# Another order for the steps behind the first key tile of a linear-attention and feed-forward kernel

## The chip, the cores and the metric

The kernel runs on one core of one Trainium2 chip. The metric is the device time of one execution in microseconds (us); a lower one is better. A core has five engines, each with an instruction stream of its own, which wait for each other through semaphores: TensorE (PE in the profile, PEld its weight loads), VectorE (DVE), ScalarE (ACT), GpSimd (POOL) and SyncE (SP), which here issues nearly all transfers and transposing transfers.

## The reference

Two residual blocks over 2048 tokens of width 640, in bf16. The first is a linear attention with 32 heads of width 20, the second a feed-forward of width 1728 with SiLU.

```
q, k, v = split(layernorm(x) @ wqkv)          # 32 heads of 20
pq, pk  = q @ w_phi, k @ w_phi                # per head, 20 x 20
phi_q   = [softmax(pq), softmax(-pq)]         # 40 features
phi_k   = [softmax(pk), softmax(-pk)]
kv, z   = phi_k^T @ v, sum over tokens of phi_k
o       = (phi_q @ kv) / (phi_q . z + 1e-6)
h       = x + o @ wo
out     = h + silu(layernorm(h) @ w1) @ w2
```

## The kernel before

The 2048 tokens are 16 tiles of 128. The program is a list of 899 named steps (`ORDER`, lines 18 to 61). Each name stands for a small function that emits the instructions of one step; they are emitted in the order of the list (lines 1097 to 1102), and each engine runs its own instructions in that order. So the list fixes the order on every engine and on SP's queue. It is written out by hand, as far as the kernel is concerned: nothing reorders it later. The number in a name is the tile, or the unit of tiles.

The first stage folds `w_phi` into the query and key weights (`wk`, `fk`, `fq`: small products on PE; `wq` is a transposing load of a query weight block, `WTq`, line 425). Then, for each tile `t`:

- `st`, `rs`, `xn`: layer norm. `st` (lines 478, 479) on DVE; `rs` on ACT or POOL; `xn` (line 494) on DVE for tiles 0, 1, 2 and 6 and on POOL for the others.
- `xt`: transposes the normalized tile into `XnT`. For tiles 0 to 3 PE does it (line 530); from tile 4 on SP issues a transposing transfer (line 552).
- `K`, `V` (line 571, ten matmuls each): keys and values; `ex` (line 626, ACT), `su` (line 630, DVE), `rk` (lines 638, 639, ACT), `sc` (line 643, DVE) make the two softmaxes of the keys in the tile `EK`; `ve` (line 647, ACT) copies the values. `kv` (line 662, eleven matmuls on PE) adds the tile to the running key-value product and needs `sc` and `ve`.
- `Q` (line 609, ten matmuls), `qe` (line 733, ACT), `qs`, `ql`, `qi`, `qr`: the query features `EQ`; `qt` (line 779) issues their transposing transfer into `EqT`.
- `bd` (lines 671, 673, DVE) cuts the finished key-value product to blocks; `D` (line 817, PE) multiplies the query features by it, `E` (lines 826, 827, DVE) divides into the tile `O`, `ot` (line 839) issues its transposing transfer into `OT`, `G` (line 849, two halves) is the output projection and `ga` (line 856, DVE) the residual.
- `lm`, `ls`, `lr`, `hn`, `ht`: the second layer norm and its transposing transfer into `HnT`.

The feed-forward works on units of two or four tiles: `u` (lines 931, 942) and `s` (lines 954, 970) are the first product and SiLU, `lt` a transposing transfer. The second product takes tiles in pairs and multiplies blocks of a 2 by 2 split with seven products instead of eight: `T` and `S` (DVE) form sums of weights and of activations, `p1` to `p7` (line 1036) are the products, `r` and `w` (lines 1044, 1051) gather them, `out` stores. The last pair's `p3` is cut into 192 and 128 columns, `p3.14` and `p3.14x`.

The weights of the later stages come through eleven loads on SP (`load0` to `load10`, line 563): `load0` is `wo` (800 KB), `load1` to `load5` are `w1` (432 KB each), `load6` to `load8` (480 KB each), `load9` (640 KB) and `load10` (80 KB) are `w2`.

Results of PE go to eight PSUM banks. While keys and values are projected, three pairs of banks are taken in turn, so a `K`, `V`, `fq` or early `Q` also waits until the step that empties its pair three takings ago (`ex`, `ve`, `fq..e`, `qe`) has run. Later (from the step `halves` on) a ring of single banks is used in the same way.

Of the kernel before, what the change touches and what calls it, by code (L numbers as in the profile page):

```python
# [26 lines left out]
ve6 fq1 st10 fq1e K7 V7 zeros rs10 su5 xt8 rk4 sc4 fq4 xt9 ex7 ve7 rs11 kv4 fq4e ref8 ones6 xn10 su6 su7
rk5 V8 ve8 V9 load4 rk7 sc5 st12 fq5 ve9 st14 rk6 xn11 rs12 K8 fq5e xt10 ref9 rs13 xn12 ex8 sc6 kv5 sc7
K9 su8 ref10 load1 V10 ex9 ve10 load5 kv6 eqr0 rs14 su9 Q0 K10 rk8 xn13 kv7 Q1 xt12 qe0 ref11 xt11 sc8
rk9 ref12 st15 sc9 xt13 xn14 kv8 rs15 K12 kv9 ex10 V12 su10 qe1 ex12 load0 K11 qs1 ve12 K13 xt14 rk10  # L30
su12 ex11 load10 qs0 ref13 V11 sc10 kv10 xn15 ex13 xt15 K14 su11 ql1 ve11 eqr1 rk12 V13 su13 qi1 ref15
eqp rk11 sc11 ql0 ref14 K15 qr1 rk13 load8 mask1 sc12 ex14 ve13 sc13 ex15 kv11 load2 Q2 V15 V14 qe2 su14
qi0 su15 rk14 qr0 rk15 load3 ve14 Q3 qt1 ve15 sc14 kv12 kv13 sc15 kv14 qe3 kv15 Q7 qs2 ql2 qe7 qi2 bd0
Q5 halves qt0 bd1 D0 qr2 D1 qe5 qs3 load9 Q4 qt2 E0 qe4 ql3 Q10 qe10 D2 E1 qs5 qi3 qr3 Q6 qe6 ot0 ot1
G00 G01 ql5 qs4 E2 Q9 ql4 ga0 qi5 G11 qe9 qt3 G10 qr5 Q11 lm0 qi4 ls0 D3 qr4 ot2 lr0 qs6 ga1 Q8 qe11 lm1
G20 E3 qs7 qr6 G21 qt5 Q12 hn0 ls1 ot3 ga2 lr1 qt4 qe8 Q13 qr7 D5 G31 E5 G30 hn1 ht0 ht1 ga3 qe12 qs8
Q14 ot5 qe13 qt6 qe14 Q15 qe15 padL0 D4 T1.0 qr8 u0.L u0.8 padL1 T1.2 E4 G50 G51 qt7 T3.0 lm2 s0.L T1.1
ga5 s0.8 lm3 u0.10 s0.10 ls2 lm5 D6 T2.2 u0.4 u0.2 ot4 E6 D7 qs9 u0.6 u0.12 T3.2 s0.2 s0.4 E7 ls5 lr2
T2.0 lt0 u0.0 s0.6 G41 qr9 qt8 ot6 s0.12 G40 D8 s0.0 hn2 ot7 T2.1 p2.0 G61 T3.1 lr5 hn5 ga4 S1.0 p1.0
S3.0 ls3 S2.0 p7.0 G60 lr3 lm4 E8 ht5 r1.0 ls4 G71 S4.0 lr4 w11.0 p6.0 ga6 hn3 T4.1 p3.0 r2.0 hn4 r7.0  # L40
T4.0 G70 p5.0 T4.2 ht2 qs10 ht3 ga7 p4.0 lm7 r3.0 ht4 qt9 w21.0 lm6 w12.0 u2.L ls7 s2.L u2.3 u2.12 w22.0
D9 u2.0 u2.4 s2.12 u2.11 qs11 s2.0 ot8 s2.3 ls6 G81 G80 u2.7 qr10 qr11 E9 s2.11 u2.6 lr6 s2.6 qs14 s2.4
qt10 ga8 qs12 u2.5 qr12 lm8 u2.8 D10 out0 ot9 E10 qt11 s2.5 u2.10 hn6 ls8 G90 s2.7 u2.1 s2.8 s2.10 u2.9
out1 G91 qr14 u2.2 qs13 qr13 qt12 ga9 ot10 D11 s2.1 lt2 E11 ht6 s2.9 s2.2 S3.2 lm9 qt13 S1.2 ot11 lr8
hn8 ls9 p2.2 ht8 p1.2 lr7 D12 r1.2 S2.2 qt14 G101 G100 p7.2 p6.2 E12 r7.2 p4.2 lr9 hn7 ht7 G110 S4.2 hn9
ga10 S3.4 r2.2 w11.2 w21.2 G111 ot12 ga11 p7.4 p5.2 w22.2 lm10 r3.2 ht9 ls10 D13 lm11 ls11 p3.2 S1.4
p1.4 G121 S2.4 lr11 u6.1 r7.4 G120 r1.4 p6.4 w12.2 E13 p4.4 s6.1 ot13 ga12 D14 r2.4 w21.4 out3 E14 lm12
p5.4 ls12 lr12 u6.L w22.4 G131 r3.4 ot14 hn11 qs15 u6.3 G130 s6.L u6.2 qr15 u6.0 u6.9 ht11 s6.2 lr10
ga13 s6.0 p2.4 lm13 s6.9 w11.4 out5 hn12 u6.7 s6.3 hn10 G140 G141 u6.11 out2 s6.7 qt15 ht12 ls13 D15
S4.4 lr13 ht10 u6.12 u6.4 u6.10 s6.11 E15 ga14 hn13 s6.4 ht13 p3.4 w12.4 u6.5 u10.L ot15 s6.10 u6.8 s6.5  # L50
u6.6 s10.L lm14 s6.12 G151 s6.6 G150 lt6 S3.6 s6.8 S1.6 u10.2 ls14 p1.6 S2.6 r1.6 ga15 lm15 p7.6 r7.6
p6.6 u10.3 s10.2 p2.6 p4.6 S4.6 u10.6 s10.3 r2.6 p5.6 u10.8 u10.11 u10.9 lr14 s10.8 w21.6 S3.8 w22.6
r3.6 w11.6 p3.6 p7.8 hn14 p1.8 S1.8 s10.6 S2.8 ht14 u10.7 r1.8 p2.8 ls15 s10.9 p6.8 s10.11 s10.7 w11.8
lt10 w12.6 r7.8 u10.0 out4 u10.1 p4.8 r2.8 p5.8 lr15 u10.4 u10.10 r3.8 hn15 s10.0 w21.8 w22.8 u10.12
ht15 s10.4 s10.10 s10.12 u10.5 s10.1 u14.2 S4.8 s10.5 s14.2 S3.10 u14.12 u14.0 p2.10 out7 p7.10 S3.12
S1.10 s14.0 p3.8 p1.10 r7.10 S2.10 S4.10 out6 u14.10 p4.10 w12.8 s14.12 u14.L r1.10 u14.4 p6.10 s14.10
w11.10 p1.12 r2.10 p5.10 w21.10 u14.6 p7.12 w22.10 S1.12 s14.4 p2.12 s14.L r3.10 r7.12 r1.12 p3.10 S2.12
out8 s14.6 p4.12 w11.12 S3.14 p6.12 w12.10 out9 u14.8 s14.8 lt14 r2.12 w21.12 out11 p5.12 w22.12 p1.14
r3.12 S4.12 p7.14 S1.14 p3.12 out10 r7.14 S2.14 r1.14 p4.14 p6.14 out13 p2.14 S4.14 r2.14 w12.12 w11.14
w21.14 p5.14 p3.14 w22.14 out12 out140 r3.14 w12.14 out15 p3.14x out141 w12.14x out142  # L60
""".split()


# [1071 lines left out]
```

## Time and profile before

| | us |
|---|---|
| median of 3 runs | 227.71 (227.59 to 228.24) |
| profiled execution, its own time | 227.59 |
| its span in the profile | 225.7 |
| PE busy | 218.2 |
| DVE busy | 173.9 |
| ACT busy | 146.1 |
| POOL busy | 70.0 |

The span runs from the first to the last instruction of the trace; times inside it are counted from its start. The granted clock of TensorE was 0.999 of full speed. A row of a timeline gives the start, the time until the end of the last instruction of the row, engine, line, operation, tiles and the number of instructions; brackets hold the engine's idle time before the row and what ended it. In the rows of waits stand the waiting engine and line, what it waited for, the total in us, how often, and the longest.

### The profile page before, as it was taken

Reading aid. Unit: us, or ns where it says so; the run is one execution under the profiler, and the core shown is the slowest. Engines: PE = TensorE matmul, PEld = TensorE weight load, DVE = VectorE, ACT = ScalarE, POOL = GpSimd, SP = SyncE. Lnnn points to the kernel's source line nnn. Section 1 sums busy time; section 2 is a strip of 40 time slices with the busy share of each in tenths; the row PEclk is TensorE's granted clock in tenths of the full one; section 3 lists DMA queues with packets and bytes.
Section 4 is the critical chain, followed back from the end, with each engine's and each line's share of the span. In section 5 each row is a group of like instructions: output and inputs, shape, how many; then the busy total and the mean of one; then the engine's idle time right before and its main releaser. Section 6 shows DMA issues by size and latency. Waiting matters only on the chain.

```text
span 225.7 us, 5046 instructions
## 1 busy us (share of the span) xinstructions
PE 218.2 (97%) x1927; PEld 154.4 (68%) x1937; DVE 173.9 (77%) x305; ACT 146.1 (65%) x321; POOL 70.0 (31%) x136
## 2 busy tenths in 40 slices
PE   6899989999999999999999999999999999999994
PEld 5777767777777677887655577655556565777773
DVE  4999988999999999999998998881435533174674
ACT  2899979999988899988275776439473532612100
POOL 7589969897400131034010321130110010000000
PEclk9999999999999999999999999999999999999999
DMA  6999984669848659874735696245310033002002
GB/s 170 292 345 162 202 98 116 183 120 198 292 94 182 128 96 143 174 102 92 148 73 144 143 154 123 61 117 109 75 23 0 11 75 87 0 23 79 32 29 87
DMA packets 68158, 26.98 MB, mean 120 GB/s; under 512 B 61159, under 2 KB 67111, under 8 KB 68007
## 3 DMA queue, kind: packets, MB, share of 16 engines
q1 hardware_dynamic: 67479, 26.65, 54.3%
q8 instruction: 15, 0.25, 0.4%
q10 hardware_dynamic: 656, 0.03, 0.2%
q14 instruction: 8, 0.07, 0.1%
HBM read 9.55 MB, written 2.62 MB: 54 GB/s over the span
## 4 chain that ended last, share of the span: by engine, by line
PE 75%; DVE 14%; DMA 5%; issue 2%; ACT 2%; DVEq 0%; ACTq 0%
PE banks L931 25%; PE banks L1036 23%; PE banks L849 10%; PE banks L571 7%; PE banks L609 5%; DVE st L478 4%; DMA XnT<-xn 3%; PE banks L817 2%; DVE EK L643 2%; DVE Sk L630 2%; DMA OT<-O 2%; DVE Sq L737 1%; DVE xn L494 1%; PE banks L662 1%; ACT EK L626 1%
## 5 line engine op out<-in xcount | busy, mean ns | idle before, releaser
L931 PE MATMUL banks<-HnT,w_sb 128*128 128x512 bf16 (+1 forms) x315 | 59.8, 335 | 0.5
L954 ACT ACTIVATE shT<-banks 128x512 bf16<-128x512 f32 (+1 forms) x53 | 30.0, 587 | 45.2 <-PE banks L931 44.8
L931 PEld LDWEIGHTS <-w_sb 128*128 128x128 bf16 x325 | 31.2, 98 | 21.1
L571 PEld LDWEIGHTS <-XnT 128*128 128x128 bf16 x300 | 28.5, 98 | 10.9 <-DMA XnT<-xn 1.3
L494 POOL TENSOR_SCALAR xn<-X,mv,rs 128x640 bf16<-128x640 bf16 x12 | 30.8, 2565 | 1.5 <-ACT rs L485 1.3
L516 POOL TENSOR_SCALAR rs<-mv 128x1 f32<-128x1 f32 x16 | 4.7, 296 | 82.8 <-ACT xn L509 82.6
L1036 PEld LDWEIGHTS <-S 128*128 128x128 bf16 x231 | 22.1, 98 | 8.5
L1036 PE MATMUL banks<-T,S 128*128 128x320 bf16 x168 | 26.2, 299 | 0.0
L1051 DVE TENSOR_TENSOR o_t<-banks,r 128x320 bf16<-128x320 f32 (+2 forms) x33 | 15.1, 476 | 13.4 <-PE banks L1036 13.1
L849 PE MATMUL banks<-wo_sb,OT 128*128 128x320 bf16 x160 | 25.0, 299 | 0.4 <-DMA OT<-O 0.4
L1044 DVE TENSOR_TENSOR r<-banks,X 128x320 f32<-128x320 f32 x32 | 15.2, 485 | 12.9 <-PE banks L1036 12.8
L737 DVE TENSOR_REDUCE Sq<-EQ 128x66 f32<-128x1320 bf16 x16 | 24.3, 1519 | 0.0
L609 PE MATMUL banks<-Wfq,XnT 128*128 128x342 bf16 (+2 forms) x160 | 22.8, 293 | 0.0
L733 ACT ACTIVATE EQ<-banks 128x342 bf16<-128x342 f32 (+2 forms) x52 | 21.6, 527 | 1.9 <-PE banks L609 1.7
L571 PE MATMUL banks<-Wfk,XnT 128*128 128x304 bf16 x150 | 21.7, 292 | 1.0 <-DMA XnT<-xn 1.0
L571 PE MATMUL banks<-Wv,XnT 128*128 128x320 bf16 x150 | 22.5, 299 | 0.0
L630 DVE TENSOR_REDUCE Sk<-EK 128x64 f32<-128x1216 bf16 x16 | 21.9, 1402 | 0.4 <-ACT EK L626 0.4
L1036 PEld LDWEIGHTS <-shT 128*128 128x128 bf16 x168 | 16.3, 98 | 6.9
L626 ACT ACTIVATE EK<-banks 128x608 bf16<-128x608 f32 x32 | 20.3, 695 | 0.8 <-PE banks L571 0.8
L849 PEld LDWEIGHTS <-OT 128*128 128x128 bf16 x160 | 15.3, 98 | 7.4 <-DMA OT<-O 0.6
L609 PEld LDWEIGHTS <-XnT 128*128 128x128 bf16 x160 | 15.0, 97 | 5.4
L504 ACT ACTIVATE xn<-X 128x640 bf16<-128x640 bf16 x16 | 11.9, 745 | 10.0 <-DVE X L856 10.0
(97 smaller groups left out, 327.1 us busy)
## 6 DMA issues: line engine op xcount, KB each, us to landing
out_dram<-o_t SPq DMA_DIRECT2D x15, 160.0 KB, 1.9
w_sb<-in_B_w_dram SPq DMA_DIRECT2D x5, 432.0 KB, 3.8
w_sb<-in_B_w_dram SPq DMA_DIRECT2D x3, 480.0 KB, 4.1
X<-in_A_x_dram SPq DMA_DIRECT2D x1, 1280.0 KB, 8.0
Wk<-in_A_wqkv_dram SPq DMA_DIRECT2D x5, 160.0 KB, 3.6
Wv<-in_A_wqkv_dram SPq DMA_DIRECT2D x5, 160.0 KB, 5.2
wo_sb<-in_A_wo_dram SPq DMA_DIRECT2D x1, 800.0 KB, 6.3
X<-in_A_x_dram SPq DMA_DIRECT2D x1, 640.0 KB, 6.3
```

The lines of the kernel that those rows point to most:

```text
L494: eng.tensor_scalar(out=xn_[t][:], in0=X[:, t, :], scalar1=mv_.pop(t)[:, 0:1], scalar2=rs_.pop(t)[:], op0=ALU.subtract, op1=ALU.mult,)
L571: nc.tensor.matmul(ps[:, g, 0:w], XnT[:, c, t * P : (t + 1) * P], W[:, c, g * w : (g + 1) * w], start=(c == 0), stop=(c == C - 1),)
L609: nc.tensor.matmul(ps[:, 0 : e - a], XnT[:, c, t * P : (t + 1) * P], Wfq[:, c, a:e], start=(c == 0), stop=(c == C - 1),)
L626: nc.scalar.activation(E5[:, :, :, b, 0:DR], p4, AF.Exp, scale=sign)
L630: nc.vector.tensor_reduce(sk[t][:], ek[t][:, 0 : H * HF].rearrange("p (q f) -> p q f", f=DH)[:, :, 0:DR], axis=AX.X, op=ALU.add)
L733: nc.scalar.activation(features(t, a, b)[:, :, :, i, 0:DR], p4, AF.Exp, scale=sign)
L737: nc.vector.tensor_reduce(sq[t][:], EQ[0][:, t, :, 0:FCH].rearrange("p c (q f) -> p c q f", f=DH), axis=AX.X, op=ALU.add)
L849: nc.tensor.matmul(ps_of["G", t][:, g, 0:HD], ot[t][:, c, :], wo_sb[:, c, g * HD : (g + 1) * HD], start=(c == 0), stop=(c == C - 1),)
L931: nc.tensor.matmul(ps[:, at : at + n], w1_sb[:, c, fc * P : fc * P + P], HnT[u][:, c, 0:n], start=(c == 0), stop=(c == C - 1),)
L954: nc.scalar.activation(rows_of(u)[:, f0 * n : f1 * n], ps_of.pop(("u", u, f0))[:, 0 : (f1 - f0) * n], AF.Silu)
L1036: nc.tensor.matmul(ps[:, lo:hi], left[:, c, :], right[:, c, lo:hi], start=(c == 0 and k in FIRST), stop=(c == KS - 1 and k in LAST), skip_ ...
L1044: nc.vector.tensor_tensor(r_[t, name][:], ps_of[bank, t][:, 0:HD], X[:, t + i, g * HD : (g + 1) * HD], op=ALU.add)
```

## The change

The same 899 steps stand in the list in another order from the 105th on; the first that moves is `wq3`. No step is added, removed or altered, and no function changes. On SP's queue the order of the transposing transfers and the loads becomes another one, on PE, DVE, ACT and POOL that of the computing steps. What the prediction speaks of:

- SP before: `X8 wq3 wq2 wq0 xt4 load7 xt5 load6 xt6 wq1 xt7 wq5 xt8 xt9 load4 xt10 load1 load5 xt12 xt11 xt13 load0 xt14 load10 xt15 load8 load2 load3 qt1 qt0 load9 qt2 ot0 ot1`
- SP after: `X8 load10 wq0 xt4 wq3 xt5 xt6 wq2 xt7 wq1 xt8 xt9 wq5 xt12 xt10 load7 load3 xt11 load9 xt13 load1 xt14 load4 xt15 load0 load2 qt0 qt1 load8 load5 load6 qt2 ot0 ot1`
- PE before, from `V0.4`: `V2 K2 V3 K3 kv0 kv1 K4 V4 fq3 V5 fq0 K5 K6 fq2 kv2 kv3 V6 fq1 K7 V7 fq4 kv4 V8 V9 fq5 K8 kv5 K9 V10 kv6 Q0 K10 kv7 Q1`
- PE after: `K2 V2 V3 kv0 K3 K4 V4 kv1 fq0 V5 fq3 K5 K6 kv2 kv3 V6 fq2 K7 V7 kv4 fq1 V8 fq4 V9 K8 K9 fq5 kv5 kv6 kv7 Q0 K10 V10 Q1`
- PE around the first `G`, before: `D0 D1 Q4 Q10 D2 Q6 G00 G01 Q9`; after: `D0 D1 Q4 Q10 Q6 D2 Q9 G00 G01`
- DVE before, from `su0`: `su0 su1 st6 st7 sc0 xn6 sc1 st11 st8 su3 su2 sc3 st9 sc2 st13 su4 st10 su5 sc4 su6 su7 sc5 st12 st14 fq5e sc6 sc7`
- DVE after: `su0 st6 su1 sc0 st7 st9 xn6 sc1 st12 st8 su2 su3 st10 sc2 sc3 su4 su5 su6 sc4 st15 st11 su7 st14 sc6 sc5 sc7 fq5e`

The head of the diff:

```diff
-wph0 K0.4 rs3 rs2 st4 K0.3 K1 V0.2 xn2 xt2 st5 ex0 rs4 ex1 V0.1 wph1 x2 V1 X8 ve1 xn3 wq3 xt3 V0.4 x3
-wq2 xn4 wq0 rs5 ve0 xn5 su0 rk0 V2 su1 st6 st7 rs6 sc0 K2 V3 xn6 rk1 ve2 xt4 ones5 rs7 K3 sc1 st11 kv0
-ex2 st8 kv1 ve3 ex3 load7 phq xt5 ones2 K4 rs8 load6 su3 ex4 rk3 xt6 su2 wq1 sc3 V4 st9 ve4 fq3 fq3e rk2
-xn7 V5 ref5 ve5 sc2 fq0 fq0e st13 rs9 K5 ref6 ex5 xn8 K6 fq2 kv2 ref7 ex6 xt7 su4 fq2e xn9 kv3 wq5 V6
...
+wph0 K0.4 rs3 rs2 st4 K0.3 K1 V0.2 xn2 xt2 st5 ex0 rs4 ex1 V0.1 wph1 x2 V1 X8 ve1 xn3 xt3 su0 st6 rk0
+xn4 V0.4 su1 x3 load10 ones5 wq0 sc0 K2 st7 rs5 st9 ve0 V2 xn5 rs6 xt4 xn6 ex2 rk1 sc1 ve2 ones2 rs9
+st12 wq3 xt5 phq V3 kv0 rs7 ve3 xt6 K3 K4 xn7 V4 ref5 kv1 ex3 ex4 st8 rs8 su2 su3 ve4 fq0 fq0e V5 fq3
+ref6 st10 rk2 xn8 ve5 wq2 K5 xn9 rk3 xt7 fq3e sc2 ex5 K6 ex6 kv2 wq1 sc3 su4 kv3 ref7 V6 su5 fq2 rk4 ve6
...
```

The list ends, before, with `p3.14 w22.14 out12 out140 r3.14 w12.14 out15 p3.14x out141 w12.14x out142`, and after with `p3.14x w22.14 p3.14 r3.14 w12.14x out13 out140 out15 out142 w12.14 out141`.

More of the change, by code (lines that the diff above doesn't have):

```diff
@@ L27 @@
[L27 to L60, printed above, removed]
+wph0 K0.4 rs3 rs2 st4 K0.3 K1 V0.2 xn2 xt2 st5 ex0 rs4 ex1 V0.1 wph1 x2 V1 X8 ve1 xn3 xt3 su0 st6 rk0
@@ new lines @@
+xn4 V0.4 su1 x3 load10 ones5 wq0 sc0 K2 st7 rs5 st9 ve0 V2 xn5 rs6 xt4 xn6 ex2 rk1 sc1 ve2 ones2 rs9
+st12 wq3 xt5 phq V3 kv0 rs7 ve3 xt6 K3 K4 xn7 V4 ref5 kv1 ex3 ex4 st8 rs8 su2 su3 ve4 fq0 fq0e V5 fq3
+ref6 st10 rk2 xn8 ve5 wq2 K5 xn9 rk3 xt7 fq3e sc2 ex5 K6 ex6 kv2 wq1 sc3 su4 kv3 ref7 V6 su5 fq2 rk4 ve6
+K7 V7 rs12 fq2e ref8 su6 xn12 sc4 kv4 fq1 rs10 ex7 ve7 xt8 st15 rk6 ones6 xt9 fq1e zeros V8 st11 su7 fq4
+xn10 st14 ref9 ve8 rs11 wq5 sc6 rk5 fq4e xt12 xt10 rk7 V9 load7 sc5 ve9 K8 xn11 K9 sc7 fq5 kv5 fq5e kv6
@@ new lines @@
+load3 kv7 ex8 ex9 st13 rs14 rs13 eqr0 su8 Q0 qe0 su9 ref10 rk8 rk9 xn13 K10 ref12 xn14 ex10 xt11 V10 sc8
+ve10 ref11 load9 Q1 kv8 V12 rs15 xn15 xt13 K12 qs0 qe1 su10 sc9 kv9 rk10 ve12 ref13 K11 load1 ex12 K13
+ex11 sc10 qs1 su12 xt14 ql0 ex13 ql1 V11 su11 su13 eqr1 rk12 rk11 load4 qi0 ve11 kv10 K14 xt15 sc11 rk13
+V13 ref14 sc12 eqp qr0 qi1 ex14 ve13 qr1 sc13 ref15 K15 load0 Q2 ex15 load2 kv11 kv12 su14 kv13 su15 V15
+qe2 qt0 rk14 qt1 rk15 V14 sc14 ve14 sc15 mask1 load8 ve15 Q3 qs2 kv14 ql2 kv15 Q5 bd0 qe3 qe5 Q7 bd1
@@ new lines @@
+load5 qi2 halves qr2 qe7 D0 D1 qs3 ql3 E0 load6 Q4 qe4 Q10 qi3 qt2 E1 qr3 qs5 qe10 qs4 ql5 Q6 qe6 ot0 D2
+ot1 Q9 qe9 qi5 ql4 qr5 E2 G00 G01 ga0 lm0 ls0 qi4 G11 G10 qt3 Q11 qs6 qr4 D3 ga1 qe11 qt5 E3 lm1 lr0 hn0
+Q8 ls1 D5 ot2 qt4 Q13 qr6 G20 qs7 lr1 G21 qe8 hn1 Q14 qe13 E5 Q15 qe14 ot3 Q12 ga2 G31 G30 ht0 qe15 qe12
+padL0 qs8 ht1 D4 u0.L ot5 T1.2 T1.0 qr7 s0.L T1.1 u0.0 lm2 padL1 qt6 ga3 E4 qt7 u0.6 qs9 G50 s0.0 qr8
+lm3 G51 T2.1 s0.6 D6 u0.4 ls2 s0.4 ga5 E6 u0.8 D7 ot4 lr2 lm5 qt8 u0.10 T3.2 u0.2 E7 G41 G40 ls5 hn2
@@ new lines @@
+u0.12 ot6 s0.2 T2.2 D8 lr5 s0.8 T3.1 T3.0 lt0 ls3 S3.0 s0.10 ga4 hn5 E8 s0.12 ot7 T2.0 p7.0 S1.0 G61
+p1.0 T4.1 S2.0 p2.0 r1.0 r7.0 G60 ht2 p6.0 T4.0 T4.2 lr3 p4.0 G71 S4.0 r2.0 p3.0 lm4 p5.0 qr9 ls4 lr4
+G70 ga6 hn3 ht5 w21.0 qs11 hn4 w22.0 ga7 ht3 ht4 u2.L lm6 u2.9 s2.L u2.1 qt9 r3.0 u2.7 ot8 w11.0 lm7
+w12.0 lt2 qr11 u2.10 s2.9 qs10 G81 qt11 s2.1 qr10 qs12 D9 u2.3 s2.3 s2.7 qt10 G80 E9 u2.5 ls6 lr6 u2.4
+s2.10 u2.2 ga8 u2.6 D10 ls7 u2.0 ot9 qr12 qt12 qs13 u2.12 s2.4 E10 lm8 D11 hn6 s2.5 ls8 ot10 u2.8 s2.0
@@ new lines @@
+qs14 E11 s2.6 s2.12 lr7 lr8 u2.11 G90 qr13 s2.2 D12 hn7 hn8 S3.2 ht6 s2.8 G91 p7.2 G101 qr14 ga9 s2.11
+S1.2 p1.2 S2.2 E12 G100 r1.2 out0 p2.2 ga10 qt13 ot11 lm9 p6.2 qt14 S4.2 D13 r2.2 r7.2 G110 G111 w11.2
+ls9 out1 S3.4 p4.2 E13 p5.2 ot12 ga11 lr9 w21.2 ht7 hn9 ht9 ht8 w22.2 ot13 D14 p7.4 r3.2 E14 lm11 p3.2
+qs15 S1.4 p1.4 S2.4 ls11 G121 r1.4 lm10 u6.L ls10 G120 u6.8 lr10 p6.4 r7.4 p4.4 ga12 S4.4 r2.4 lm12 qr15
+G131 w12.2 ot14 w21.4 G130 ga13 qt15 s6.L hn10 ls12 ht10 p5.4 lr11 s6.8 u6.11 G140 lm13 hn11 s6.11 u6.4
@@ new lines @@
+s6.4 lr12 D15 G141 u6.2 hn12 ls13 out3 r3.4 w22.4 p2.4 u6.5 s6.5 s6.2 E15 ga14 lr13 hn13 u6.1 w11.4 ht12
+u6.0 u6.3 lt6 u6.10 u6.7 out2 s6.10 s6.7 s6.3 s6.1 p3.4 w12.4 ht11 ht13 u6.6 s6.0 u10.L ot15 u6.12 u10.2
+s6.12 u10.9 s10.L G151 G150 s6.6 u6.9 S3.6 s10.2 u10.11 s6.9 S1.6 ga15 S2.6 lm15 u10.0 p7.6 s10.9 p1.6
+u10.6 lt10 lm14 S3.8 r1.6 s10.0 r7.6 s10.11 u10.7 s10.6 s10.7 u10.12 p4.6 S4.6 p6.6 p2.6 s10.12 r2.6
+p5.6 r3.6 ls15 w11.6 w21.6 u10.5 p2.8 S1.8 ls14 u10.3 w22.6 out5 lr15 u10.1 s10.5 p7.8 lr14 p1.8 S2.8
@@ new lines @@
+s10.3 hn14 u10.4 hn15 s10.1 r1.8 s10.4 ht14 w11.8 S3.10 p3.6 p6.8 ht15 r7.8 S4.8 u10.8 p4.8 out4 u14.4
+r2.8 w21.8 w12.6 s14.4 u10.10 p5.8 s10.8 w22.8 p3.8 r3.8 out6 u14.2 out9 w12.8 s14.2 s10.10 S1.10 u14.12
+p7.10 u14.10 out7 u14.L s14.12 u14.0 u14.6 p1.10 out8 S3.12 s14.0 s14.L r7.10 lt14 u14.8 S2.10 r1.10
+s14.6 p6.10 p4.10 s14.10 r2.10 p5.10 w21.10 r3.10 S4.10 p2.10 p7.12 p2.12 w11.10 w22.10 S1.12 p1.12
+S2.12 r1.12 w11.12 p3.10 p6.12 r7.12 p4.12 S4.12 r2.12 S3.14 w21.12 s14.8 w12.10 p5.12 p1.14 out11 r3.12
@@ L61 @@
+p7.14 S1.14 p3.12 S2.14 p2.14 r1.14 p6.14 w22.12 r7.14 out10 S4.14 w12.12 p4.14 r2.14 p5.14 w21.14
+w11.14 out12 p3.14x w22.14 p3.14 r3.14 w12.14x out13 out140 out15 out142 w12.14 out141
 """.split()
```

## The prediction

> **What bounds the kernel now.** I read the page's busy times first, then what TensorE (PE) waited for, then PE's timeline at those waits, then the chain.
>
> ```profile
> span 225.7 us, 5046 instructions
> PE 218.2 (97%) x1927; PEld 154.4 (68%) x1937; DVE 173.9 (77%) x305; ACT 146.1 (65%) x321; POOL 70.0 (31%) x136
> PE banks L571 <- DMA XnT<-xn: 1.0, 1, 1.0
> PE banks L849 <- DMA OT<-O: 0.4, 1, 0.4
> ```
>
> PE is the bound, and the order changes none of its work. Of its waits only two stand behind the first moved step (wq3): one on a transposed tile XnT, one on a transposed OT. So the question is how much of these goes, and what new waits come. The timeline of PE prices them, and gives the prices of its steps:
>
> ```profile
> 15.98 0.43 PE L583 MATMUL banks<-Wv,XnT 128*128 128x320 bf16 x2
> 22.23 1.45 PE L571 MATMUL banks<-Wfk,XnT 128*128 128x304 bf16 x10
> 23.52 1.52 PE L571 MATMUL banks<-Wv,XnT 128*128 128x320 bf16 x10
> 24.88 0.41 PE L437 MATMUL banks<-phi_q,WTq 128*128 128x114 bf16 x5
> ...
> 26.55 0.41 PE L437 MATMUL banks<-phi_q,WTq 128*128 128x114 bf16 x5
> 26.80 1.45 PE L571 MATMUL banks<-Wfk,XnT 128*128 128x304 bf16 x10
> 29.26 1.47 PE L571 MATMUL banks<-Wfk,XnT 128*128 128x304 bf16 x10 [1.01 <-DMA XnT<-xn]
> ...
> 30.82 0.84 PE L662 MATMUL banks<-VP,EK 128*128 128x63 bf16 x22
> 31.50 0.70 PE L571 MATMUL banks<-Wv,XnT 128*128 128x320 bf16 x4
> ...
> 69.31 0.88 PE L817 MATMUL banks<-KVB,EqT 128*128 128x63 bf16 x24
> 70.03 2.77 PE L609 MATMUL banks<-Wfq,XnT 128*128 128x342 bf16 x20
> ...
> 73.00 1.47 PE L609 MATMUL banks<-Wfq,XnT 128*128 128x342 bf16 x10
> 74.83 1.53 PE L849 MATMUL banks<-wo_sb,OT 128*128 128x320 bf16 x10 [0.36 <-DMA OT<-O]
> ```
>
> Ends are modelled, so a step's price is the distance of starts: K 1.29 (22.23 to 23.52), V 1.36, fq 0.25, kv 0.34 (two in 0.68), D 0.36 (two in 0.72), Q 1.31 (two and a D from 70.03 to 73.00); V0.4, two of a V's ten matmuls, 0.27. K6 should have followed K5 at 26.80 + 1.29 = 28.09 and came at 29.26: the first wait cost 1.17. G00 should have come at 73.00 + 1.31 = 74.31 and came at 74.83: the second cost 0.52. Together 1.69 us; the rest of PE's idle time lies before wq3 or behind its last product.
>
> Why the two tiles came late:
>
> ```profile
> 23.10 6.12 DMA XnT<-xn
> 71.21 3.57 DMA OT<-O
> XnT<-xn SPq DMA_TRANSPOSE x12, 2.8
> OT<-O SPq DMA_TRANSPOSE x16, 2.6
> 21.16 1.21 SPq L552 DMA_TRANSPOSE XnT<-xn  x1
> 22.41 0.59 SPq L563 DMA_DIRECT2D w_sb<-in_B_w_dram  x1
> 23.10 1.21 SPq L552 DMA_TRANSPOSE XnT<-xn  x1
> ...
> 26.45 2.05 SPq L552 DMA_TRANSPOSE XnT<-xn  x1
> ```
>
> xt6 took 6.12 us to land against a median of 2.8; 0.7 us ahead of it stands a weight load (load6). ot0 took 3.57 against 2.6 with no load near. The DMA rows of two short stretches (26.2 to 28.3 and 71.8 to 73.2) show the other neighbour, one packet of an instruction queue, while the engines' busy share falls to 0 or 1 tenth:
>
> ```profile
> DMA  9999999999992990919009101010101010001999
> q8 instruction: 1, 0.02, 3.1%
> ```
>
> ```profile
> DMA  0090000000000000134889999999999999999999
> q8 instruction: 1, 0.02, 5.3%
> ```
>
> **The change part by part.** No instruction is added or removed; 795 of 899 steps stand behind the first moved one. I lay PE's new order end to end, which gives each step a due time, and compare what feeds it.
>
> *The early transposes.* In the new order load6 and load7 leave the place around xt5 and xt6, and SP issues xt4, wq3, xt5, xt6, wq2, xt7, wq1, xt8, xt9, wq5, xt12, xt10 with no load between. K6 is due at 15.98 + 0.27 + K2 to K5 5.16 + V2 to V5 5.44 + kv0, kv1 0.68 + fq0, fq3 0.50 = 28.03. xn6, on VectorE (DVE), moves behind st9:
>
> ```profile
> 14.73 2.61 DVE Sk L630 x2
> 17.34 0.81 DVE st L478 x2
> 18.16 0.21 DVE mv L479
> ...
> 19.29 0.88 DVE EK L643
> 20.16 0.36 DVE xn L494
> 20.52 0.73 DVE EK L643
> ```
>
> So su costs 1.31, st 1.02, sc 0.73 to 0.88. xn6 ends at 14.73 + su0, su1 2.61 + st6, st7, st9 3.06 + sc0 0.88 + 0.36 = 21.64, 1.1 us later than before; xt5's issue (21.16 to 22.37) hides that, and xt6 goes out at 22.4. It lands at 25.2 by the median and 28.5 by the worst row: 2.8 us to spare, or 0.5 short. I take the median, since load6 is gone and its flight ends before the fetch at 26.3. The 1.17 goes.
>
> *wq3, wq2, wq1 move behind transposes.* Their landing takes up to 6.4:
>
> ```profile
> WTq<-in_A_wqkv_dram SPq DMA_TRANSPOSE x6, 6.4
> ```
>
> wq3 goes out behind xt4 at about 18.9, lands by 25.3; fq3 is due at 26.49. wq2 goes out at 23.6, lands by 30.0; fq2 is due at 31.36. wq1 goes out behind xt7's issue, about 28.5 as the WTq did that stood there, and lands by 34.9; fq1 is due at 34.60. Cost 0, at most 0.3.
>
> *DVE's queue.* PE now comes 1.2 us earlier to steps that DVE feeds, and DVE is given st9, st12, st10, st15 earlier than before. kv3 is due at 28.03 + 1.29 + 0.34 = 29.66. DVE in front of it: 14.73 + su0 to su3 5.24 + six st 6.12 + sc 0.88 + 3 x 0.73 + xn6 0.36 = 29.52. kv4 is due at 31.61 (K7: 28.03 + 1.29 + 0.68 + 1.36 + 0.25) + 1.29 + 1.36 = 34.26; DVE adds su4, su5, su6 and sc4, 4.66, and is there at 34.2. kv7 is due at 41.33 (kv4 0.34, fq1, fq4, fq5 0.75, V8, V9 2.72, K8, K9 2.58, kv5, kv6 0.68 behind 34.26); DVE adds st15, st11, st14 3.06, su7 1.31, sc6, sc5, sc7 2.19, and is there at 40.7. But there sc ran longer, and DVE had waited:
>
> ```profile
> 34.90 0.83 DVE L643 TENSOR_TENSOR EK<-EK,Rk 128x1280 bf16<-128x1280 bf16 x1 [1.56 <-ACT Rk L639]
> 38.30 1.34 DVE L643 TENSOR_TENSOR EK<-EK,Rk 128x1280 bf16<-128x1280 bf16 x1
> 41.81 1.82 DVE L643 TENSOR_TENSOR EK<-EK,Rk 128x1280 bf16<-128x1280 bf16 x2
> ```
>
> With 1.34 + 1.82 for the three, DVE is there at 41.7, 0.4 late. The wait of 1.56 was for rk4, which stood on ScalarE (ACT) behind ve6, and so behind V6 and the late K6; the new order puts rk4 before ve6, and K6 is early. I take it as gone. Sum for DVE: 0.1 each at kv3 and kv4, where nothing is to spare, and 0.1 of the 0.4 at kv7: 0.3; bounds 0 and 2.5 (the third rival). ACT has as many steps as before ahead of ex4, which frees V5's bank (rs9 stands in for rs8): 0.
>
> *xn12 before xn10 on POOL.* xt10 is then behind xn8, xn9, xn12, xn10:
>
> ```profile
> L494 POOL TENSOR_SCALAR xn<-X,mv,rs 128x640 bf16<-128x640 bf16 x12 | 30.8, 2565 | 1.5 <-ACT rs L485 1.3
> ```
>
> 26.45 + 4 x 2.57 = 36.7, and 39 with 2.3 that I allow for POOL's small steps and waits; landed by 41.8. K10 is due at 41.33 + 0.34 + 1.31 = 42.98. Cost 0.
>
> *ot0 and G00.* From D0's start to G00's, 5.52 us passed before, wait included. In the new order D0, D1, Q4, Q10, Q6, D2 and now Q9 too stand between: 3 x 0.36 + 4 x 1.31 = 6.3. ot0 even with 3.57 is there 0.8 early: the 0.52 goes (it stays if DVE reaches E0 0.8 late).
>
> *The end.* The 128 columns of the last product come before its 192; the same DVE steps and as many stores follow. 0.
>
> *Behind 105 us* each PE step has its feeder moved with it; I allow 0.2 for places not worked out.
>
> Sum against the profiled execution's own 227.59: 227.59 - 1.17 - 0.52 + 0.3 + 0.2 = 226.4. The median of the three runs is 227.71, 0.12 higher: **226.5 us**.
>
> The instruction packets bear on the first rival. The Trainium skill, page "Runtime: NRT & Kernel Launch", section "Instruction fetch mechanics", says that a sequencer fetches its next 16 KiB through its own DMA queue while it runs, and that this is mostly hidden. For the fetching engine the trace agrees (no PE wait is put down to it); for a neighbour it does not: ot0, alone with one packet of q8, took 3.57 instead of 2.6. By the rule, keeping transposes off these places would be worth nothing, xt7 (next paragraph) would land at 29.3, and the sum would stay.
>
> **The rivals.**
> 1. *The fetch at 26.3 now meets xt7.* xt7's issue is bound by POOL's xn7 to 26.45 in both orders, and K7 is due 1.5 us earlier, at 31.61. With 6.12 it lands at 32.57: 0.96 late, 227.4. For: an instruction packet moves just there. Against: less stands ahead of xt7, and wq1 now comes behind it.
> 2. *Transposes are not kept apart later on.* Behind xt10 the new order issues load7, load3, xt11, load9, xt13, load1, xt14. load9 (640 KB) just ahead of xt13 is what load6 was to xt6: out at 46.4 (xt10's 39, two more xn 5.1, 2.3 again), landed with 6.12 by 52.5; K13 is due at 42.98 + 3 K 3.87 + V10, V12 2.72 + Q1 1.31 + kv8, kv9 0.68 = 51.56. 1.0 late, 227.5. Against: 2.4 to spare with 2.8.
> 3. *DVE is the bound, and PE comes early for nothing: slower.* sc7 ended at 43.63 before, 2.9 us behind DVE's sum. If none of this was K6's fault, kv7, due at 41.33, waits 2.3; with 0.2 at kv3 and kv4: 226.0 + 2.5 = 228.5. It decides against the change from 1.7 us of new waits on. For: between its rows above DVE hardly rests. Against: 1.56 of the 2.9 followed K6.
>
> **How the numbers follow.** Forecast 0.55 (own range 225.9, nothing new at all, to 226.9); first rival 0.12; second 0.10; third 0.17; 0.06 for waits I could not place. A measurement of this kernel can tell about 0.3%, 0.68 us, from no change: faster is below 227.03, slower above 228.39. Of the first two rivals, which can also cost less, 0.04 end below 227.03. Faster 0.55 + 0.04 = 0.59; within 0.18 + 0.03 = 0.21; slower 0.17 + 0.03 = 0.20. The range 225.8 to 228.4 leaves out the third rival's upper part and some of what I could not place.
>
> **What would show it.** Right: no PE wait on XnT near 28 or on OT near 74, xt6 landing in about 3 us, K6's start near 28.0 and D0's near 68.2 instead of 69.31, PE's last product 1.2 us or more earlier. Wrong: PE waits on EK (L643) at L662 between 29 and 42 (third rival), on XnT near 31.6 (first) or 51.6 (second), or on a feeder behind 105 us.

## The result and the profile after

| | before | after |
|---|---|---|
| median of the four runs of each in this comparison, us | 227.65 (227.46 to 228.24) | 226.22 (225.95 to 226.34) |
| profiled execution, its own time | 227.59 | 226.19 |
| its span | 225.7 | 224.5 |

The ratio of the times is 0.9931, with a 95% interval of 0.9911 to 0.9952. 1.43 us went; 226.5 us, which is 1.21 below the median known then, had been forecast. The span is 1.2 us shorter; the other 0.2 of the profiled execution's 1.40 lies around the span. The profiled execution of e7, a repeat of the changed kernel that comes further down, was one of the slower kind (clock 0.991, 229.39 us against that kernel's 226.28), so its span is not compared.

First the page of the changed kernel and what PE waited for in it (waiting engine, tile and line, what it waited for, the total in us, how often, the longest):

```profile
span 224.5 us, 5053 instructions
PE 219.7 (98%) x1937; PEld 155.1 (69%) x1937; DVE 173.9 (77%) x305; ACT 144.8 (65%) x321; POOL 72.5 (32%) x136
PE banks L231 <- PEq L1119: 0.8, 1, 0.8
PE banks L345 <- ACT rs L484: 0.3, 1, 0.3
PE banks L662 <- DVE EK L643: 0.2, 1, 0.2
```

That list of waits is complete. The waits for `XnT` (L571) and for `OT` (L849) are gone; one of 0.2 for `EK` at a `kv` (L662) is new. L231 and L345 lie in the first stage, ahead of the first moved step. PE's 219.7 against 218.2 is no added work. The trace of before lacks ten of PE's matmul records (x1927 against x1937), which is about 0.5 of the 1.5. The rest lies in the first 15.5 us, where the same 127 instructions are busy for 14.24 instead of 13.19 us; both kernels reach `V0.4`, the last step of PE ahead of the change, at the same time (15.98 and 15.96).

Then PE's timeline at the two places (start, length of the row, engine, line, operation, tiles, number; in brackets the idle time before):

```profile
26.72 2.75 PE L571 MATMUL banks<-Wfk,XnT 128*128 128x304 bf16 x20
29.30 0.50 PE L662 MATMUL banks<-VP,EK 128*128 128x63 bf16 x11
30.00 0.51 PE L662 MATMUL banks<-VP,EK 128*128 128x63 bf16 x11 [0.20 <-DVE EK L643]
...
33.25 1.52 PE L571 MATMUL banks<-Wv,XnT 128*128 128x320 bf16 x10
34.73 0.51 PE L662 MATMUL banks<-VP,EK 128*128 128x63 bf16 x11
...
41.01 1.17 PE L662 MATMUL banks<-VP,EK 128*128 128x63 bf16 x33
...
68.61 0.88 PE L817 MATMUL banks<-KVB,EqT 128*128 128x63 bf16 x24
...
73.60 1.47 PE L609 MATMUL banks<-Wfq,XnT 128*128 128x342 bf16 x10
74.90 2.88 PE L849 MATMUL banks<-wo_sb,OT 128*128 128x320 bf16 x20
77.62 0.60 PE L609 MATMUL banks<-Wfq,XnT 128*128 128x342 bf16 x3
```

Before, `K5` and `K6` were two rows 2.46 us apart; now they are one row of 20 matmuls, and `K6` starts at 26.72 + 1.29 = 28.01 instead of 29.26. `kv3` is late: 29.30 + 0.34 = 29.64 was its place, it came at 30.00. `kv4` could have come at 33.25 + 1.36 = 34.61 and came at 34.73. So of the 1.25 us at `K6`, `D0` (L817) keeps 0.70 (68.61 against 69.31). The row of 20 at L849 is `G00 G01 G11 G10` (five matmuls each), and it follows `Q9` without a gap. With these five done, PE goes on with `Q11` at 77.62; before, where the order was `G00 G01 Q9 G11 G10`, the same point was reached with the start of this row:

```profile
78.86 1.35 PE L609 MATMUL banks<-Wfq,XnT 128*128 128x342 bf16 x9
```

1.24 us earlier: 0.70, and 0.54 at `G00`. Behind that nothing is won or lost: the end also comes 1.2 earlier, and the view by stretches has PE busy all the time from 68 to 216 us (columns: stretch, its length, busy us of PE, PEld, DVE, ACT and POOL with their instructions, clock, DMA share, GB/s):

```profile
68.00:105.00 37.00, 37.00 (x384) 29.20 (x382) 36.16 (x60) 34.94 (x88) 8.77 (x23) 1.00 0.70 134
105.00:216.00 111.00, 111.00 (x838) 71.22 (x836) 70.44 (x134) 51.04 (x101) 11.56 (x31) 1.00 0.37 75
```

The transposes, from SP's timeline and from the DMA view of 0.1 to 0.3 us around an issue (count of issues, time to landing):

```profile
21.47 2.55 SPq L552 DMA_TRANSPOSE XnT<-xn  x2
...
27.10 1.21 SPq L552 DMA_TRANSPOSE XnT<-xn  x1
```

```profile
XnT<-xn SPq DMA_TRANSPOSE x1, 2.6
```

This row is that of a stretch from 22.7 to 23.0: `xt6`, the second of the two issued together from 21.47 on, takes 2.6 us instead of 6.12. The stretch around 27.1 (`xt7`) answers with the same row. `ot0`, in the stretch from 70.4 to 70.6, does not:

```profile
OT<-O SPq DMA_TRANSPOSE x1, 3.6
```

So `ot0` is as slow as it was (3.57); only what stands ahead of `G00` on PE hides it now.

### The profile page after: what moved, and what is told of

Its sections match the earlier page's. It is cut to its first block, busy times and chain, and to the rows that moved or that the text cites. A ratio compares the mean times of both kernels' runs of the same rounds, so it can differ in the third digit from the quotient of the medians.

```text
span 224.5 us, 5053 instructions
## 1 busy us (share of the span) xinstructions
PE 219.7 (98%) x1937; PEld 155.1 (69%) x1937; DVE 173.9 (77%) x305; ACT 144.8 (65%) x321; POOL 72.5 (32%) x136
## 4 chain that ended last, share of the span: by engine, by line
PE 87%; DVE 11%; issue 0%; DVEq 0%
PE banks L931 25%; PE banks L1036 23%; PE banks L571 11%; PE banks L849 10%; PE banks L609 9%; DVE st L478 4%; PE banks L817 3%; DVE Sk L630 2%; PE banks L662 2%; PE banks L231 2%; DVE xn L494 1%; DVE EK L643 1%; PE banks L942 1%; DVE mv L479 1%; DVE WTk L338 0%; PE banks L437 0%
## 5 line engine op out<-in xcount | busy, mean ns | idle before, releaser
L931 PE MATMUL banks<-HnT,w_sb 128*128 128x512 bf16 (+1 forms) x325 | 60.7, 336 | 0.0
L954 ACT ACTIVATE shT<-banks 128x512 bf16<-128x512 f32 (+1 forms) x53 | 29.5, 587 | 32.1 <-PE banks L931 31.9
L571 PEld LDWEIGHTS <-XnT 128*128 128x128 bf16 x300 | 28.7, 98 | 9.6
L494 POOL TENSOR_SCALAR xn<-X,mv,rs 128x640 bf16<-128x640 bf16 x12 | 32.4, 2701 | 1.6 <-ACT rs L485 1.3
L516 POOL TENSOR_SCALAR rs<-mv 128x1 f32<-128x1 f32 x16 | 3.5, 219 | 80.2 <-ACT xn L509 79.9
L1036 PEld LDWEIGHTS <-S 128*128 128x128 bf16 x231 | 22.1, 98 | 9.0
L1044 DVE TENSOR_TENSOR r<-banks,X 128x320 f32<-128x320 f32 x32 | 15.2, 486 | 15.9 <-PE banks L1036 15.5
L1036 PE MATMUL banks<-T,S 128*128 128x320 bf16 x168 | 26.7, 299 | 0.0
L849 PE MATMUL banks<-wo_sb,OT 128*128 128x320 bf16 x160 | 25.3, 299 | 0.0
L609 PE MATMUL banks<-Wfq,XnT 128*128 128x342 bf16 (+2 forms) x160 | 22.7, 293 | 0.0
L571 PE MATMUL banks<-Wv,XnT 128*128 128x320 bf16 x150 | 22.5, 299 | 0.0
L571 PE MATMUL banks<-Wfk,XnT 128*128 128x304 bf16 x150 | 21.2, 292 | 0.0
L849 PEld LDWEIGHTS <-OT 128*128 128x128 bf16 x160 | 15.3, 98 | 6.4
```

What stands on the lines that cost most here:

```text
L494: eng.tensor_scalar(out=xn_[t][:], in0=X[:, t, :], scalar1=mv_.pop(t)[:, 0:1], scalar2=rs_.pop(t)[:], op0=ALU.subtract, op1=ALU.mult,)
L571: nc.tensor.matmul(ps[:, g, 0:w], XnT[:, c, t * P : (t + 1) * P], W[:, c, g * w : (g + 1) * w], start=(c == 0), stop=(c == C - 1),)
L609: nc.tensor.matmul(ps[:, 0 : e - a], XnT[:, c, t * P : (t + 1) * P], Wfq[:, c, a:e], start=(c == 0), stop=(c == C - 1),)
L849: nc.tensor.matmul(ps_of["G", t][:, g, 0:HD], ot[t][:, c, :], wo_sb[:, c, g * HD : (g + 1) * HD], start=(c == 0), stop=(c == C - 1),)
L931: nc.tensor.matmul(ps[:, at : at + n], w1_sb[:, c, fc * P : fc * P + P], HnT[u][:, c, 0:n], start=(c == 0), stop=(c == C - 1),)
L954: nc.scalar.activation(rows_of(u)[:, f0 * n : f1 * n], ps_of.pop(("u", u, f0))[:, 0 : (f1 - f0) * n], AF.Silu)
```

## The experiments

Two theories were set against each other throughout. One: the gain is the two waits, each with its own cause (the loads beside `xt6`; `ot0` late with too little in front of `G00`), and the other 790 or so moved steps do nothing. The other: the rearranged queues of VectorE, ScalarE and POOL carry a part. Each kernel below is the order of before or the changed order with a few steps moved. The ratio is to the kernel before on the same chip; "K6" and "G00" are what PE lost there in the profiled execution.

| run | order, with this moved | median, us | ratio (95%) | span | K6 | G00 |
|---|---|---|---|---|---|---|
| before | | 227.65 | 1 | 225.7 | 1.17 | 0.52 |
| after | | 226.22 | 0.9931 (0.9911 to 0.9952) | 224.5 | 0 | 0 |
| e1 | before, load6 and load7 away | 226.27 | 0.9943 (0.9914 to 0.9973) | 224.3 | 0 | 0.46 |
| e4 | after, load6 and load7 back | 228.00 | 1.0034 (0.9994 to 1.0073) | 225.7 | 2.07 | 0 |
| e10 | before, load6 away | 226.46 | 0.9934 (0.9908 to 0.9961) | 225.3 | 0 | 0.85 |
| e11 | before, load7 away | 227.34 | 0.9986 (0.9966 to 1.0006) | 226.1 | 1.56 | 0.46 |
| e2 | before, Q9 ahead of G00 | 227.51 | 0.9976 (0.9937 to 1.0015) | 225.4 | 0.62 | 0 |
| e6 | after, Q9 and qe9 back | 227.21 | 0.9962 (0.9924 to 1.0000) | 225.5 | 0 | 0.58 |
| e5 | before, more PE instructions in front | 228.68 | 1.0055 (1.0027 to 1.0083) | 226.5 | 0.24 | 0 |
| e3 | after, DVE's order near kv3 changed | 226.76 | 0.9951 (0.9932 to 0.9970) | 225.0 | 0 | 0 |
| e9 | after, st9 behind xn6 | 226.29 | 0.9928 (0.9903 to 0.9954) | 224.6 | 0 | 0 |
| e8 | before, e1 and e2 together | 226.64 | 0.9951 (0.9925 to 0.9978) | 224.6 | 0 | 0 |
| e7 | after, unaltered, once more | 226.28 | 0.9928 (0.9896 to 0.9960) | | 0 | 0 |

**The loads near xt6: e1, e4.** e1 takes the order of before and moves only the two loads:

```diff
-ex2 st8 kv1 ve3 ex3 load7 phq xt5 ones2 K4 rs8 load6 su3 ex4 rk3 xt6 su2 wq1
+ex2 st8 kv1 ve3 ex3 phq xt5 ones2 K4 rs8 su3 ex4 rk3 xt6 su2 wq1
...
-V9 load4 rk7
+V9 load4 load7 rk7
...
-ex11 load10 qs0
+ex11 load10 load6 qs0
```

> The order of before, but load7 goes out behind load4 and load6 behind load10, so no load stands near xt5 and xt6. Theory A (the load ahead of xt6 and the instruction packet at 26.3 together made it late): xt6 lands in 2.6 to 3 us, before the packet, the PE wait on XnT before K6 is gone and the time falls by 1.2 us, to about 226.5; the 0.5 us wait for OT before G00 stays. Theory B (the packet alone made xt6 late, the load does not matter): xt6 still takes 4 us or more and K6 waits over 0.5 us. Theory C (PE's time is given back to DVE later): the wait goes, but new PE waits on EK at L662 of together 0.5 us or more come before 60 us, and the time falls by less than 0.7.

e4 is the reverse: the changed order with `load7` ahead of `xt5` and `load6` ahead of `xt6`.

> The changed order, but load7 goes back in front of xt5 and load6 in front of xt6. Theory A (load and packet together): xt6 lands after 5 us or more, K6 waits 0.5 to 1.3 us on XnT, and the time rises from 226.2 to 226.7 to 227.5. Theory B (the packet alone, and xt6 left its place because DVE and SP moved): xt6 lands in 3 us or less, no wait on XnT, 226.2.

In e1 the wait at `G00` stays, as expected: `ot0` went out at 69.80 and landed at 73.38, and `G00` came at 73.42. (The list of waits puts this one down to ScalarE, but the bank that `G00` needs had been empty since 71.05.) The DMA view of the stretch from 22.0 to 22.1 has `xt6` at 2.6, and PE runs through from `K5` to `K6`:

```profile
XnT<-xn SPq DMA_TRANSPOSE x1, 2.6
```

```profile
26.51 2.74 PE L571 MATMUL banks<-Wfk,XnT 128*128 128x304 bf16 x20
```

In e4 `xt6` takes 6.8, and PE waits:

```profile
XnT<-xn SPq DMA_TRANSPOSE x1, 6.8
```

```profile
26.44 1.46 PE L571 MATMUL banks<-Wfk,XnT 128*128 128x304 bf16 x10
29.80 1.47 PE L571 MATMUL banks<-Wfk,XnT 128*128 128x304 bf16 x10 [1.91 <-DMA XnT<-xn]
```

`K6` lost 29.80 - 26.44 - 1.29 = 2.07, more than the 1.17 of before: `xt6` went out as early as in before (22.96 against 23.10) but took 6.80 instead of 6.12, and PE was due at `K6` 0.36 earlier. The size of this wait differs from one execution to the next; with the loads in their old places it was 0.62 in e2, 1.17 in before and 2.07 here. Moving two of 899 steps gives the changed kernel's time within the intervals (0.9943 against 0.9931), and moving them back takes all of it away. On this wait the first theory holds: the loads' places, not the engines' new orders, are worth the larger part. That the other moved steps do nothing is not so, as e6 and e8 below show.

**Which of the two: e10, e11.** e10 moves `load6` alone, e11 `load7` alone.

> The order of before with load6 alone behind load10; load7 stays ahead of xt5. If load6, issued 0.7 us ahead of xt6, is what delays xt6: xt6 lands in 2.6 to 3.6, K6 waits 0.1 or not at all, the span is 224.4 to 224.7 and the time 226.3 to 226.6. If both loads together fill the 16 engines, xt6 still takes 4 to 5 (load7's data reaches into its flight), K6 waits 0.2 to 0.8.

> The order of before with load7 alone behind load4; load6 stays ahead of xt6. If load6 is what delays xt6: xt6 takes 5 to 6, K6 waits 0.6 to 1.2 as before, the time is 227.3 to 227.7. If both loads together fill the engines: xt6 4 to 5, K6 waits 0.2 or nothing, the time is 226.4 to 226.8.

In e11 the wait stays, in e10 it is gone (the two kernels' PE timelines at `K6`, e11 first, and the stretches around `xt6`'s issue):

```profile
29.71 1.47 PE L571 MATMUL banks<-Wfk,XnT 128*128 128x304 bf16 x10 [1.39 <-DMA XnT<-xn]
```

```profile
XnT<-xn SPq DMA_TRANSPOSE x1, 6.5
```

```profile
27.23 2.74 PE L571 MATMUL banks<-Wfk,XnT 128*128 128x304 bf16 x20
```

```profile
XnT<-xn SPq DMA_TRANSPOSE x1, 5.2
```

`load6`, the load directly ahead of `xt6` on SP, makes the wait. But e10 also shows the second part of the matter: with `load7` two places ahead, `xt6` still takes 5.2; a packet of q8, out at 25.05, also fell into its flight. It does no harm because it goes out at 22.08 instead of 23.10, partly because `load6`'s 0.6 us on SP are gone, and lands at 27.25, ahead of `K6` at 28.5. e10's span has not the whole gain because `G00` lost 0.85 there, and `V5` 0.44 waiting for ScalarE.

**Q9 in front of G00: e2, e6.** e2 is the order of before with `Q9` moved from behind `E2` to ahead of `G00`; e6 is the changed order with `Q9` back behind `G01` and `qe9` behind `G11`.

> The order of before, but Q9 goes in front of G00. Theory A (G00 lacked only PE work in front of it): ot0 lands in about 3.6 us as before, G00 no longer waits, the time falls by 0.5 us to about 227.1, and the wait of 1.2 us before K6 stays. Rival: Q9 must wait for its PSUM banks (qe10) or G00 for its own, and the 0.5 us only changes its name: within 0.2 us of before.

> The changed order, but Q9 goes back behind G01 (and qe9 behind G11, since it reads Q9). Theory A: ot0 lands at about 74.1, G00 is due 1.3 us earlier, at 73.75, and waits 0.3 to 0.5 us: 226.5 to 226.7. Rival (ot0 is early enough by itself in the new order): no wait, 226.2.

In e2 `G00` starts at once, and the wait comes up again 26 us later at `D8`, whose query features were in flight:

```profile
75.02 2.88 PE L849 MATMUL banks<-wo_sb,OT 128*128 128x320 bf16 x20
...
100.94 0.53 PE L817 MATMUL banks<-KVB,EqT 128*128 128x63 bf16 x12 [0.52 <-DMA EqT<-EQ]
```

The wait at `K6` stays, smaller than expected (0.62), so the time is 227.51 and not 227.1. In e6 the wait at `G00` comes back with 0.58, and 0.42 that was not foreseen comes at `Q14`, which waited for the bank of `Q8`, emptied by `qe8` on ScalarE:

```profile
74.16 1.53 PE L849 MATMUL banks<-wo_sb,OT 128*128 128x320 bf16 x10 [0.42 <-DMA OT<-O]
...
84.59 4.08 PE L609 MATMUL banks<-Wfq,XnT 128*128 128x342 bf16 x30 [0.25 <-ACT EQ L733]
```

The span of e6 is 1.0 longer than that of the changed kernel, and 0.58 + 0.42 is 1.0. So `Q9`'s place ends the wait at `G00`, but it keeps the gain only where the steps behind it are in place too. e8, with e1's and e2's edits together, has no wait at `G00`, but 0.22 at `D8`, as e2 had, and 0.41 at `V10`; its span is 224.6 where 223.9 had been expected. The 0.41 is not `Q9`'s doing: `load7`, in its new place behind `load4`, stands directly ahead of `xt10`, which took 4.3 us instead of 3.1 (a packet of q8 was in its flight too).

> The order of before with load7 and load6 moved away and Q9 in front of G00. If the two waits are separate and the rest of the reordering does nothing, this has all of the gain: e1's span of 224.3 less its 0.46 at G00, 223.9, and a time of 225.7 to 225.9. If the cover that Q9 gives at G00 only moves the wait (e2 lost 0.68 at D8 for qt8), it stays at e1's 226.3, with a wait of 0.4 to 0.7 on EqT near 100.

**The instruction packet in ot0's flight: e5.** Twenty warm-up matmuls of 256 columns became forty of 128, so that PE's instruction packets are asked for about 40 instructions sooner; the order is that of before.

```diff
-WARM = 20
+WARM = 40
...
-kv_ps[:, 0, 0 : 2 * P], warm_t[:, 0:P], warm_t, start=True
+kv_ps[:, 0, 0:P], warm_t[:, 0:P], warm_t[:, 0:P], start=True
```

> The order of before with the 20 warm-up matmuls of 256 columns replaced by 40 of 128 columns (their result is not used). This puts 40 more instructions into PE's stream in front of everything, so that each later instruction packet of PE's queue comes some 40 instructions, 2 to 3 us, earlier: the one at 71.9 comes at about 69.5 and no longer meets ot0. Theory A (the packet makes a transpose that it meets about 1 us later): ot0 lands in 2.6 us, G00 does not wait (0.5 us less), and qt2, which the packet meets now, takes about 4 us instead of 3.1; near xt6 the packet comes at about 24, still beside load6, and the wait before K6 stays between 0.3 and 1.2. Theory B (the packet does nothing to a neighbour, as the rule has it that fetching is hidden): ot0 still takes 3.6 us and G00 waits 0.5 us.

In before the packet of q8 starts 0.7 us behind `ot0`'s issue (71.90 against 71.21), ahead of the transpose's own data. In e5 it starts with the issue (71.58 against 71.61) and is over, after 0.88 us, before `ot0`'s data moves. It had been expected at 69.5, well ahead of `ot0`; this packet came only 0.3 us earlier, though others came 0.6 to 4 us earlier (26.30 became 22.86, 62.28 became 61.66). So `ot0` got free of it by a narrow margin. The DMA view of e5 from 71.55 to 71.70:

```profile
q8 instruction: 1, 0.02, 36.8%
...
OT<-O SPq DMA_TRANSPOSE x1, 2.6
```

2.6 instead of 3.57, and no wait for `OT`. But now the packet falls into the flight of the transpose ahead of it, `qt2`, out at 69.08: that takes 4.6 instead of 3.1, and `D2` waits for it. Likewise the packet that now starts at 35.50 falls into `xt9`'s flight, which takes 4.4 with no load ahead, and PE waits for that until 38.1 (lines stand two lower in this kernel):

```profile
PE banks L573 <- DMA XnT<-xn: 0.7, 1, 0.7
PE banks L819 <- DMA EqT<-EQ: 0.6, 1, 0.6
```

The kernel is 0.55% slower than before. Moving the packets alone moves the waits.

**DVE in front of kv3: e3, e9.** e3 takes `st12` and `su6` out of DVE's way, behind `sc3` and `sc4`; e9 puts `xn6` ahead of `st9`.

> The changed order, but on DVE st12 goes behind sc3 and su6 behind sc4, so that sc3 and sc4 are done earlier. Theory A (what is left of PE's waits behind the first key tile is DVE's queue in front of kv3 and kv4, 0.35 and 0.12 us): both waits go and the time falls by 0.4 us from 226.2 to 225.8. Rival (DVE is the bound further on): the waits turn up again at kv5 to kv7 near 41 us, 226.2. Second rival: rs12 or rk6, which follow the moved steps on ACT, hold ACT up and with it a bank: slower than 226.3.

> The changed order with st9 behind xn6, so that VectorE runs xn6 1.0 us earlier and outside the end of POOL's xn5. If kv3's 0.35 comes from xn6 taking 0.96 instead of 0.36 there, xn6 takes 0.4, xn5 2.5 instead of 2.76, kv3's wait falls to 0.1 or nothing, and the time is 225.8 to 226.0. If VectorE is simply full in front of kv3 and xn6 takes as long wherever POOL has an xn beside it, xn6 stays at 0.8 to 1.0, the wait stays at 0.2 to 0.35 and the time at 226.2.

e3 has no gap at `kv3` (its PE timeline) and loses elsewhere: 0.30 at `V7` and 0.40 at `V12`, both waiting for ScalarE, as the second rival had it; 1.08 in all gaps ahead of 60 us against 0.60 in the changed kernel. The row of waits below is that of `V12`.

```profile
29.32 0.84 PE L662 MATMUL banks<-VP,EK 128*128 128x63 bf16 x22
...
33.20 1.52 PE L571 MATMUL banks<-Wv,XnT 128*128 128x320 bf16 x10
```

```profile
PE banks L571 <- ACT EK L626: 0.2, 1, 0.2
```

In e9 (DVE's timeline) `xn6` is as long as in the changed kernel. But this doesn't show that its place is indifferent: the move took it from the end of POOL's `xn5` to just behind its start (19.48), and the last section shows that both are slow places:

```profile
19.59 0.94 DVE L494 TENSOR_SCALAR xn<-X,mv,rs 128x640 bf16<-128x640 bf16 x1
```

The gap at `kv3` is gone there, but not through `xn6`: in this execution PE reached `K5` 0.41 later than in the changed kernel's (27.13 against 26.72), and DVE reached `su1`, which stands ahead of the moved step, 0.43 earlier (16.53 against 16.96). `kv4` lost 0.24 instead of 0.12, and the time is the same, 226.29. So neither edit of DVE's order wins anything. The last run repeats the changed kernel unaltered, beside e8 and e9:

> The changed order as it is, beside the next two. Both theories: 226.2 us, a span of 224.5, TensorE waiting behind kv2 for EK (0.2 at kv3, as often as once), no wait for XnT near 28 and none for OT near 74.

Its 226.28 lies with the first 226.22. Whether the gap at `kv3` comes in every execution of the changed kernel is not shown: e6, whose steps are the same up to there, lost 0.35 at `kv3` again. No version tried beats the changed kernel by more than the runs differ; e1, with two steps moved, equals it.

## Why the prediction was right

**The wait at K6, -1.17.** Right in size and cause. The row showed 6.12 us for `xt6` with `load6` ahead of it; e11 against e10 shows that `load6` makes the wait. `xt6` was said to go out at 22.4 and land at 25.2; SP issued it at 22.8 (21.47 plus the first of the two issues), and with 2.6 it landed at 25.4. `K6` was due at 28.03 and came at 28.01.

**The wait at G00, -0.52.** Right: 0.54. `ot0` kept its 3.6, as assumed when only the cover was counted. What the prediction didn't see is how little `Q9`'s move does by itself: it was costed as a step that only takes a wait away, while alone in the order of before it makes `D8` wait (0.68 in e2, 0.22 in e8).

**DVE's queue, +0.3.** The sign and the place were right and the size too small: 0.36 at `kv3` and 0.12 at `kv4`, against 0.1 each, and two gaps under 0.1 near 50 and 59 us that weren't foreseen. The sum for `kv3` had counted 0.36 for `xn6`; the chain of waits shows what it took:

```profile
21.00 0.96 DVE xn L494
21.96 0.88 DVE EK L643
...
28.52 1.44 DVE EK L643 x2
...
30.00 0.51 PE banks L662 x11
```

`sc2` and `sc3` (L643) end at 29.95 instead of the 29.52 that the sum gave, and `xn6`'s 0.60 more is the part of that which can be named; the last section shows what it depends on. At `kv7` 0.1 had been charged, because `sc6`, `sc5` and `sc7` were priced at the 1.34 + 1.82 of the rows of before. They took 2.25 in all:

```profile
38.95 2.25 DVE L643 TENSOR_TENSOR EK<-EK,Rk 128x1280 bf16<-128x1280 bf16 x3
```

In before the two long ones had begun 0.20 us (38.30) and 0.46 us (41.81) behind the start of an `xn` on POOL, and those of the changed kernel did not. They ended at 41.20, `kv5` to `kv7` stand in one row from 41.01 on, and nothing was lost.

**Places behind 105 us, +0.2.** Nothing was lost there (111.00 of 111.00 us busy). So the new waits came to 0.60 (0.36, 0.12, 0.05, 0.08) against the 0.5 allowed for them, in part at other places: the sum gave a span of 225.7 - 1.19 = 224.5, and 224.5 was measured. The two waits were worked out; that the allowances for the rest came out so close is luck. That the median came 0.3 below the forecast is the 0.2 around the span, and 0.1 because the median stands 0.03 above the profiled execution and not 0.12.

**Terms costed at nothing.** `wq3`, `wq2` and `wq1` landed in 3.0, 4.9 and 3.1 us, and PE waited for none of them. `wq1` went out at 28.4, as said, and landed at 31.5, 3.6 ahead of `fq1` at 35.08. `K10` did not wait for `xn12` and `xt10`.

**The rivals.** *The fetch meets xt7*: false. `xt7` went out at 27.10, since POOL ran `xn7` 0.65 us later than before, and took 2.6; the packet of q8 had moved to 25.09, 0.3 us before `xt6` was down, and was over (1.39) before `xt7` went out. The prediction had left that packet at 26.3 without working out its new place; that it fell between the two transposes' data is luck. *load9 ahead of xt13*: the mechanism was there, its price was not. SP's timeline, and the DMA view around 46.5:

```profile
44.69 0.58 SPq L563 DMA_DIRECT2D w_sb<-in_B_w_dram  x1
46.45 1.21 SPq L552 DMA_TRANSPOSE XnT<-xn  x1
```

```profile
XnT<-xn SPq DMA_TRANSPOSE x1, 5.0
```

It was out at 46.45, as predicted (46.4), but took 5.0 instead of 6.12, and landed at 51.5; `K13` came at 51.96 and had 0.5 us to spare. With 6.12 it would have waited 0.6. In e6 and e9, with `load9` in the same place, `xt13` took 3.2, so even the 5.0 does not come each time. *DVE is the bound*: false. It would have cost 2.5 us; 0.48 came at `kv3` and `kv4`, and none at `kv7`.

**The rule on instruction fetch.** The changed kernel's time doesn't decide it, since `xt6` met only the first 0.3 us of a packet of q8 there and `xt7` none. e5 does: `ot0` takes 2.6 with the packet out of its flight and 3.6 with it inside, and `qt2` goes from 3.1 to 4.6 where it meets one. The Trainium skill, page "Runtime: NRT & Kernel Launch", section "Instruction fetch mechanics", calls the cost of a block boundary mostly hidden; that holds for the engine that fetches, but not for a transpose in flight beside it.

## What to carry to other kernels

Look at what stands directly ahead of a soon-needed transpose in its queue: a weight load there that nothing needs for a long time cost 1.2 us here, and moving two steps of 899 won as much as the reordering of them all. Price a move by what it pushes as well as by what it frees: here putting PE work in front of a late transpose, shifting instruction packets, and giving DVE another order each ended one wait and started others. A sum that leaves 0.1 us to spare on a second engine should take the longer of the durations that its operations show, since the trace of before had DVE's `xn` at 0.43 for one tile and at 0.81 for another.
